# State increments in the four column quarters of the array, and a new issue table

## The chip, the cores and the metric

The kernel runs on one core of one Trainium2 chip. The metric is the device time of one execution in microseconds. TensorE (PE in the profile) does the matrix products, VectorE (DVE), ScalarE (ACT) and GpSimd (POOL) the elementwise work, and SyncE (SP) issues the transfers between memory and the core.

## What is computed

A linear attention with a decaying state, and behind it a gated feed-forward layer that mixes along the sequence. Cut to the core:

```python
# attention: 4 batches, 8 heads, 768 steps, head size 48
for t in range(S):
    cur = einsum('bhd,bhe->bhde', u * k[t], v[t])
    y[t] = einsum('bhd,bhde->bhe', r[t], state + cur)
    state = w[t][..., None] * state + einsum('bhd,bhe->bhde', k[t], v[t])
x = y as [4, 768, 384]
# gated layer: 384 -> 1024, halves u and v, mix along the sequence, 512 -> 384
h = maximum(x @ w_in, 0);  u, v = halves of h
v_n = (v - mean(v)) / sqrt(var(v) + 1e-6)
v_s = einsum('ts,bsd->btd', w_spatial, v_n) + b_spatial[None, :, None]
out = (u * v_s) @ w_out
```

## The kernel before

**Tiles.** The sequence of each batch is cut into 6 chunks of 128 steps, so there are 24 slots i (batch b, chunk c). In a slot the decay products come from two scans on DVE (`slot_prep`, lines 414 and 422: tiles `F` and `pa`), which scale `kk` and `rr`. Two heads stand one above the other in 112 partitions, so 4 pairs g cover the 8 heads.

**A slot on TensorE** is a row of blocks. `slot_kt` (L492) transposes `kk`. `slot_a` (L472, `pa<-rr,kk`) forms the scores of the chunk, both heads of a pair at once in two row halves of the array. DVE copies the masked scores into the tiles `As` (L477). `slot_y` (L512, output `pyw`) has three blocks: two *intra* blocks that multiply `As` with `v` (8 matmuls each) and, in all chunks but the first of a batch, an *inter* block with the state `Sd` (12 matmuls); their outputs are 32 columns wide, so four of them work side by side in the four column quarters of the array. `slot_s` (L550, `pd<-v,KT`) forms the state's increment: for each pair one product of 64 and one of 48 columns, side by side in two column halves, 8 matmuls in all. DVE, POOL and ACT then update the state `Sd` (L556 to L566). `slot_x` (L579 to L587) takes the output apart into a high and a low part.

**The gated layer on TensorE.** `hv_unit` (tile `ph`) forms the v half of a chunk, `g_unit` the u half (`pu`) and the mix along the sequence (`pv`), `out_unit` the last product (`po`). Each product is three matmuls with the full array (L592 to L594). The mix of a batch waits until all its six chunks are normalised (tiles `vh`, `vl`).

**Records.** A matmul of plain 32-bit floats stands in the profile as two records, one of the three of L592 to L594 as one. So the `pd` block is 16 records, an intra block 16, an inter block 24, a `pa` block 16.

**What sets the order.** All work is written down as 1805 operations with their dependences. `PLAN` has for each the engine it runs on (T, V, A, G, S for TensorE, DVE, ACT, POOL, SP) and a start time; `plan()` sorts by it, and each engine executes its own operations in just that order. An engine whose next operation isn't ready waits. Buffers are few (two each of `W`, `kk`, `rr`, `v`), so a load waits in SP's queue for the slot two before to be done with its buffer, and what stands behind it waits too.

**Filler.** `fill` puts matmuls on zeros (`warm`, L791, `pyw<-zk`) in the order wherever the table leaves TensorE idle for over 0.3 us, up to the operation `last`; they hold up TensorE's clock. They write a part of the tile `pyw`, in which the outputs stand.

The modes of the array are named in the code: `full` (128 by 128), `rows` (`pa`), `halves` (`pd`), `quadrants` (`pyw` of `slot_y`).

Of the kernel before, what the change touches and what calls it, by code (L numbers as in the profile page):

```python
# [15 lines left out]
B, H, S, D = 4, 8, 768, 48  # L16
# [3 lines left out]
R = 112  # L20
# [13 lines left out]
A31t V38b V3b7 V3qe A5sz V5zd S4hn V4t4 V5p1 V5tw V5vj A5yu G60x S3s4 A46d V4vn V5aj V5c6 A5eu G5gh S3bd
A3rr V4fl V4im V4wm A4zg G52v T1xf T2yw T30u A33g A35r A37u Sdt Sbp S9k Sjw Gli Tpr Vmc Vug Vv0 Vvk V120
A12k Gqx V12h Au1 Guw Gyk G10c T14z V1ba V18s Ttn V111 G124 A13p A14o Tvd Awz T1e2 T1fe T1go A1k9 T1m8 A1pe
T1zd T2wx T386 A3br A3fo A3gb Shr Ssp Sqk S19d G13j T18j V14d G17x V1at V1ep V1qb A1sg G18m V1i9 A1ct G1i9
G1ep G1gh T1re V1zr V21s Tz3 V17t G1c4 A1ja A1n0 T1cu A1eg T22e T27x T298 A2ck T2iv A2k0 T2uz T32t T34r A3ir
A3l2 A3lp A3t6 V4dc V4b3 G4bm V4du G4ee G4f1 V4gk A4h6 A4ng V4r7 V4k5 A4lr G4no V4h4 A4xr V50y S1b7 S1n1
S1it S1gy G1zr T241 V1t5 G23b V272 V27n V2b3 A2dw G272 V2bk A28a G1pc A28y A2g5 T2e3 V2in V2kn T1iw V1pc  # L40
G2gx A2lc A2mb T2bg V2dh T2lw T2na T2sr A2vp T37o A3vp T4b3 T4f0 T4gy A4jk A4tb A4tz S1kx S1xo S2bc S29e
G2k8 T2ov V2f7 V2yj V2z2 V2zn V353 A37a G326 V336 A2tf G2ic A2x1 G2yz T3ae V3gw V3dx T2h5 V2mo G30r V35o
A36b T36q A3aa T3xq T3z1 T40c A451 T4ei A4fu T4va T4x8 T4z7 A529 A54j A557 S2dg S2ix S2vf S2or G3dx T3i6
V3ix G3ns V3tv V3ux V3ug A3zw G3tv V3yg V3mg A30n A3o5 A40g T42k V492 V472 T3dg V3fx G3xe A4ev A442 T4kx
T4m8 T4nj A4qk T4us A4wf T515 T534 T552 A57o A59z A5am A5e1 G5dq V5fg V5g0 V5jw V5kf V5ky V5lh V5m1 A5oa
V5q2 V5nj A630 V659 A5m1 A5pz V5rz T5vo S3ly A3x1 S40n A4ao S4e0 A5ix S5ly A5vz T3ls T3n9 T45m A47s T5sr
T5u7 T60b T61s T6ew T6gd V6ih G6k4 A6n3 G6pp T3op T3q6 T4d1 A5hl T5xe T5yv T638 T64p T6aj T6ht V6k0 G6mx
A6pv G6si T3rm T3t3 T48j A4dj T5vy T6ja T6kq T6m7 T6nn T6p4 V6yh V7hn A7ly V7xl T3uj T3w0 T473 A497 T665
T67m T692 T6bz T6dg T6tq V75v G77x A7c4 V7u5 T80e T81v T83b T84s V87o S89e T7yy T8ki T8lz T8nf V8qt S8u5
T7xh T868 T87p T895 A8b9 S8cr T571 T58h T59y A5g9 T6v7 T6wn T6y4 T79a T7aq T7c7 V7oj V7z5 A84l V9co T5dm  # L50
T5f3 T5ij A61o T8ow T8qc T8uq T8y1 T8zi T90y V99d G9f8 A9it V9me T5k0 T5pu T5ra A5ue T9zu Ta1b Ta2r Ta48
Ta5o Taci Vaeo Gai7 Aal5 Gasc T5lg T5mx T5od A5ro T8rt T8t9 T9pn T9r3 T9sk T9u0 V9xi G9z5 Aa3u Va5i Ta93
Taux Tb6c Tb7t Ab9x Sbbe Tbo4 Tbpk Tbr1 Tbsh Vbul Sbwb Tas0 Tatg Tbuw Tbwc Abyg Sbzy S339 S3f0 S44a S5z0
S4ad V40j G472 V4ea V4ln V4ev A50v V455 V4p7 V6a9 V6bx V6dk G4ln A6f5 A6ir T4rq V6lk V6nk T4a0 V4bl T6qu
T6s5 A6u4 T6zk A70q T73e T75d T77b A79x A7dj A7e7 S3yj S46f S4pn S6f8 S4np V52v G58b V596 V6pl V59r A6t5
V56f V6t4 V712 V72q V74d A51f A75y G765 T70c V7a4 V783 T4j7 V4y6 G594 A5d2 V5x3 T5be V5dq T7dx T7f8 T7gj
A7j5 T7l4 A7nd T7qo T7sm T7vj A7y5 A80f A860 S4rr S4ws S4uo S761 S6vb V6v1 G6yl V701 V7ca V70l A7gn V7fq
V7j7 G7j7 G7m4 V7q3 G749 G80o A80z T7lw V898 V85n T5gt V5ix G6zd A7op A7po T7ir A7kh T8cm T8dx T8f8 A8jr
V8ma T92f T94d T96c A98y A9b8 A9gd A9lk V9ix V9ny G9r8 G9rv G9si Va72 Va7m Vad6 Aaer Vaoi Va9n Aab9 Gaeo
Va85 Aacy Gakz S6t7 S73a S7ju S7rr S7i1 V7l3 G7oy V7sk V8be V7vp A8ey G7pn V8ey V82g V844 V8ou G7vp G8qf  # L60
A8qf T8hg V8sd V8ue T7oy V7rl V7t6 A8ht A8is T7ul A7w6 T8wg T98k T99v A9nc V9ou Ta75 Taak Tbga Abl0 Abna
Abny S7fw S7ou S8hc S8qi S8jg V8gu V8nt V8od V8we V8qc A8zy V8ke V8zy G90j V95u V97v G8s7 G9aw A9bs T9l4
V9qe Vab5 T8aw V9aw V9e8 A9md A9fe Tahb Aaiw Tan6 Taoh Taps Aat1 Vav5 Tb2f Tb4e Tb99 Abbv Abe6 Abhl S8f0
S8la S9ez S99j S9d6 V91v V95e V97e V9sk V9oe A9w4 G97e V9z2 G9jk G9oe V9w0 G9t2 A9yx Aapf Tae9 Vaho Vat5
Talg Vanj Gav4 Vawq Vaxg Taxl Tayw Tb07 Ab2t Vb48 Tbi8 Tbk7 Tbm5 Abqe Abso Abtc Abvv Vc0z Vbyh Vbz1 Gc1h
Gc25 Gc2s Gc54 Acih Ackt Vcqn Acd3 Acfg Gchd Ac5u Ac87 Gca4 S9yb Aa8c Sabd Aamk Sapl Aazm Sb4g Abeq T9c3
T9dk T9vh A9xl Tckn Tcm3 Tcnk Tcuu Tcwb Tcxr Vd5s Vdfo Adlz Gdnm T9f0 T9gh T9hx A9k8 Tcqh Tcrx Tcte Tcz8
Td0o Td25 Vdh8 Ve5i Ae7g Vehp T9je T9wx T9ye Aa2i Tccx Td6r Td88 Td9o Te8k Tea0 Veci Gee6 Aeio Veks T9o6
Tai9 Tajp Aaud Tcee Tcfu Tcp0 Tdm8 Tdno Tdp5 Vdup Gdys Ae61 Vej9 Teom Tewb Tf3n Tf54 Vfbr Sfff Terj Tfzn
Tg13 Tg2k Vg8h Sga6 Tglp Tgn5 Tgom Tgq2 Vgs6 Sgtw Tbxt Tca0 Tcbh Ach5 Tefu Teha Telp Ten5 Teq2 Tfde Vffi  # L70
Vflk Afo4 Vfs9 Tbz9 Tc73 Tc8k Acb8 Tgrj Tgsz Tgug Th38 Th4o Th65 Vh89 Gh9w Ahij Ghml Tc0q Tc26 Tc3n Ac9w
Tgvw Tgzd Th0t Thg7 Thhn Thj4 Vhmw Vhpe Ahr1 Ghts Tdjb Tdkr Tebh Aedl Thbt Thda Theq Thkk Thm1 Thnh Vhqy
Vhy4 Aihs Gime Tiu3 Tivk Tix0 Tiyh Vj10 Sj2q Tisn Tj4b Tj5r Tjei Ajgm Sji4 Tir6 Tizx Tj1e Tj2u Aj5g Sj6y
S900 Sah7 Sat8 Sbip Savd Va0y Va4i Va51 Vajv Vb3n Ab48 Vaqf Vb1r Gbsq Gbvn Vbzh Gb3k Ac12 Gc3c Tbbi Vc4s
Vcda Tawd Aaxz Td3v Td56 Ad75 Vd9d Tdql Tdsk Tdui Adx4 Ae2x Ae3l S9w6 Sajb Sb2b Sc1s Sb0d Vb5r Vb9b Vbbn
# [47 lines left out]
Q = 32  # L123
# [802 lines left out]
```

## Time and profile before

| | |
|---|---|
| three runs | 387.41, 386.57, 386.63 us; median 386.63 |
| profiled execution, span | 386.2 us (the median of the runs is 0.4 us above it) |
| TensorE busy | 372.1 us, 96% |
| DVE, ACT, POOL busy | 260.1, 195.5, 140.2 us |
| filler records on TensorE | 128 of 3586 |
| instructions in the table on V, A, G, T, S | 468, 372, 180, 605, 180 |

The span reaches from the first to the last instruction. The profiler's records give the start and the end of each instruction; matmuls overlap, so the time that a block costs is read from its start to the start of the next block.

### The profile page before, as it was taken

To read this page: it belongs to the slowest core of one execution; us is meant where nothing else is said; L and a number is where in the kernel's file an instruction comes from. 1 tells how busy PE (TensorE), PEld (TensorE's weight loads), DVE (VectorE), ACT (ScalarE), POOL (GpSimd) and SP (SyncE) were. 2 spreads that over 40 slices of the span, in tenths; PEclk is the share of its full clock that TensorE was granted. 3 is DMA by queue.
4 is the path that set the end of the run, shared out by engine and by line. 5 is a ranking of instruction groups with operands and counts; after the bars stand their busy time and mean duration, and the time that the engine had idled before them with its cause. 6 is when DMAs were issued, how large, how long until landed. Compare 5 with 4: busy or idle time off the path is not lost.

```text
span 386.2 us, 9096 instructions
## 1 busy us (share of the span) xinstructions
PE 372.1 (96%) x3586; PEld 338.6 (88%) x3586; DVE 260.1 (67%) x477; ACT 195.5 (51%) x514; POOL 140.2 (36%) x195
## 2 busy tenths in 40 slices
PE   8989999999999999999999999999999999999993
PEld 7778797899888898799898989899998899999992
DVE  5879987878978886377887964775697525244240
ACT  2456588785563555772454544663146535641210
POOL 5656374413540634153543313442483003300010
PEclk9989999999999999999999999999999999999997
DMA  8988548614346336533453573132265410010102
GB/s 203 277 215 251 157 138 247 205 42 122 113 133 193 112 104 180 174 108 100 123 155 85 174 208 120 50 98 86 65 177 153 118 51 0 5 38 21 63 2 70
DMA packets 33011, 47.67 MB, mean 123 GB/s; under 512 B 3264, under 2 KB 21824, under 8 KB 32960
## 3 DMA queue, kind: packets, MB, share of 16 engines
q1 hardware_dynamic: 32960, 47.00, 41.6%
q8 instruction: 30, 0.49, 0.6%
q14 instruction: 21, 0.17, 0.2%
HBM read 42.27 MB, written 4.72 MB: 122 GB/s over the span
## 4 chain that ended last, share of the span: by engine, by line
PE 77%; DMA 11%; ACT 5%; DVE 3%; POOL 1%; issue 1%; SPq 0%; ACTq 0%; POOLq 0%; DVEq 0%
PE pv L592 9%; PE pv L594 8%; PE pv L593 8%; PE pyw L512 7%; PE pa L472 5%; DMA Nw<-in_gt_dram 5%; PE po L592 4%; PE po L594 4%; PE po L593 4%; PE pu L592 4%; PE ph L592 4%; PE pu L594 3%; PE pu L593 3%; PE ph L593 3%; PE ph L594 3%; PE pyw L791 3%
## 5 line engine op out<-in xcount | busy, mean ns | idle before, releaser
L592 PE MATMUL pv<-ws,vh 128*128 128x384 f32 x192 | 65.6, 342 | 0.0
L594 PE MATMUL pv<-ws,vl 128*128 128x384 f32 x192 | 64.4, 335 | 0.0
L593 PE MATMUL pv<-ws,vh 128*128 128x384 f32 x192 | 64.3, 335 | 0.0
L477 DVE COPY_PREDICATED As<-mask,pa 128x512 f32<-128x512 int32 x48 | 34.4, 731 | 10.3 <-PE pa L472 4.0
L592 PEld LDWEIGHTS pv<-ws,vh 128*128 128x128 f32 x192 | 36.0, 188 | 1.5 <-issue 0.6
L593 PEld LDWEIGHTS pv<-ws,vh 128*128 128x128 f32 x192 | 36.1, 188 | 0.2
L698 DVE TENSOR_TENSOR t<-pv,b_sb 128x384 f32<-128x384 f32 x32 | 17.7, 553 | 27.6 <-PE pv L594 27.3
L458 ACT ACTIVATE As<-ident,dg 128x128 f32<-128x128 f32 x100 | 31.8, 390 | 8.6 <-DVE dg L438 5.4
L594 PEld LDWEIGHTS pv<-ws,vl 128*128 128x128 f32 x192 | 36.0, 188 | 0.0
L414 DVE TENSOR_TENSOR_SCAN F<-zz,W 112x512 f32<-112x512 f32 x24 | 29.2, 1217 | 7.1 <-DMA W<-in_tr_dram 3.1
L592 PE MATMUL pu<-xT,wi 128*128 128x384 f32 x96 | 33.5, 349 | 0.1
L702 ACT CAST gh<-t 128x384 fp32r<-128x384 f32 x32 | 16.3, 510 | 33.9 <-DVE t L700 29.2
L592 PE MATMUL po<-wo,gh 128*128 128x384 f32 x96 | 33.1, 344 | 0.0
L594 PE MATMUL po<-wo,gl 128*128 128x384 f32 x96 | 32.3, 337 | 0.0
L594 PE MATMUL pu<-xT,wi 128*128 128x384 f32 x96 | 32.3, 336 | 0.0
L593 PE MATMUL po<-wo,gh 128*128 128x384 f32 x96 | 32.3, 336 | 0.0
L593 PE MATMUL pu<-xT,wi 128*128 128x384 f32 x96 | 32.2, 335 | 0.0
L592 PE MATMUL ph<-wi,xT 128*128 128x512 f32 x72 | 29.6, 411 | 0.9 <-ACT ph L624 0.9
L422 DVE TENSOR_TENSOR_SCAN pa<-zz,W 112x512 f32<-112x512 f32 x24 | 29.5, 1228 | 0.6
L593 PE MATMUL ph<-wi,xT 128*128 128x512 f32 x72 | 28.3, 393 | 0.0
L594 PE MATMUL ph<-wi,xT 128*128 128x512 f32 x72 | 28.3, 393 | 0.0
L453 POOL TENSOR_SCALAR_AFFINE_SELECT As<-dg 128x512 f32<-128x512 f32 x23 | 14.8, 648 | 36.8 <-DVE dg L438 15.8
(182 smaller groups left out, 856.3 us busy)
## 6 DMA issues: line engine op xcount, KB each, us to landing
N<-in_nat_dram SPq DMA_DIRECT2D x18, 384.0 KB, 3.1
Nw<-in_gt_dram SPq DMA_DIRECT2D x16, 384.0 KB, 3.6
W<-in_tr_dram SPq DMA_DIRECT2D x24, 224.0 KB, 3.1
kk<-in_tr_dram SPq DMA_DIRECT2D x24, 224.0 KB, 3.0
rr<-in_tr_dram SPq DMA_DIRECT2D x24, 224.0 KB, 3.4
v<-in_nat_dram SPq DMA_DIRECT2D x24, 192.0 KB, 3.5
out_dram<-ot SPq DMA_DIRECT2D x24, 192.0 KB, 2.7
wst<-in_w_spT_dram SPq DMA_DIRECT2D x12, 192.0 KB, 4.3
```

The costliest lines, as they stand in the source:

```text
L414: op({"V": 1.24}, lambda: nc.vector.tensor_tensor_scan(flat(F()[:R])[:, ::-1], flat(zz[:R])[:, ::-1], flat(W())[:, ::-1], 0.0, ALU.max, AL ...
L422: op({"V": 1.24}, lambda: nc.vector.tensor_tensor_scan(flat(E()[:R]), flat(zz[:R]), flat(W()), 0.0, ALU.max, ALU.mult), r=[(W, 0), ("zz", ...
L453: e.affine_select(out=As(), in_=dg()[:, j::2].unsqueeze(2).broadcast_to([P, G, C]), pattern=[[0, G], [1, C]], compare_op=ALU.is_equal, fil ...
L458: e.mul(As()[:, g, :], ident, dg()[:, 2 * g + j:2 * g + j + 1])
L472: nc.tensor.matmul(pa[j]()[:, g, :], kk()[rs, g, :], rr()[rs, g, :], start=True, stop=True)
L477: op({"V": 0.725}, lambda j=j, As=As: nc.vector.copy_predicated(As(), mask.unsqueeze(1).broadcast_to([P, G, C]), pa[j]()), r=[(pa[j], 0)], ...
L512: nc.tensor.matmul(py()[Q * n:Q * (n + 1), k_, :], a, b, start=n not in started, stop=not left[0], skip_group_check=True)
L592: nc.tensor.matmul(ps, ah, bh, start=first, stop=False)
L593: nc.tensor.matmul(ps, ah, bl, start=False, stop=False)
L594: nc.tensor.matmul(ps, al, bh, start=False, stop=last)
L698: op({"V": dve(HT)}, lambda: nc.vector.tensor_tensor(t1(), pv()[:, :HT], b_sb[:, tsl], ALU.add), r=[(pv, 0), ("b", 0)], w=[(t1, 0)])
L702: op({"A": act(HT)}, lambda: nc.scalar.copy(gh(), t1()), r=[(t1, 0)], w=[(gh, 0)])
```

## The change

Three things are edited. The increments `pd` are cut into pieces of at most 32 columns (32, 32, 32 and 16 for a pair), so that they use the four column quarters like the outputs: 16 matmuls instead of 8. The table `PLAN` is a list of operations in the order of issue instead of start times, and another order; it has the filler in it as words F with a count, and `fill` is gone. The planned costs of some TensorE blocks are other numbers; they are used by nothing in the kernel at run time.

```diff
 PLAN = """
-T0 S72 S8b S24n S266 S14i A1fx V1k5 V1le V1nf A1qq G1t5 Sut A16z V1ym V240 V2pp A2rq V2tj S1st A242 V25x
...
+Sq T0 Vw Sr Ss S2 S1 St Vx S42 A15 S41 S43 S1w Vy S2c Vu G12 Vz S44 V10 A11 V13 Fm Tv A14 V47 S55 T1b G17 T18
...
     def plan(self):
...
+        for w in PLAN.split():
+            if w[0] == "F":
+                order.append(int(w[1:], 36))
+            else:
+                o = self.ops[int(w[1:], 36)]
+                o.on = w[0]
...
-        op({"T": 1.0}, mm, r=[(kk, 0), (rr, 0), (rr, 1)], w=[(pa[0], 0), (pa[1], 0)], mode="rows")
+        op({"T": 0.89}, mm, r=[(kk, 0), (rr, 0), (rr, 1)], w=[(pa[0], 0), (pa[1], 0)], mode="rows")
...
         def mm():
             for g in range(G):
-                for j in range(2):
-                    hs = slice((2 * g + j) * D, (2 * g + j + 1) * D)
-                    rows = slice(64 * j, 64 + j * D)
+                for q4 in range(4):
+                    hs = slice((2 * g + q4 // 2) * D, (2 * g + q4 // 2 + 1) * D)
+                    rows = slice(Q * q4, min(Q * (q4 + 1), R))
                     nc.tensor.matmul(pd()[rows, g, :], KT()[:, g, rows], v()[:, hs], start=True, stop=True)
 
-        op({"T": 0.52}, mm, r=[(KT, 0), (v, 0)], w=[(pm_, 0), ("ds", i)], mode="halves")
+        op({"T": 0.4}, mm, r=[(KT, 0), (v, 0)], w=[(pm_, 0), ("ds", i)], mode="quadrants")
...
     def issue(order):
         for o in order:
-            o.fn(ENG[o.on]) if o.fn.__code__.co_argcount > len(o.fn.__defaults__ or ()) else o.fn()
-
+            if isinstance(o, int):
+                warm(o)
+            else:
+                o.fn(ENG[o.on]) if o.fn.__code__.co_argcount > len(o.fn.__defaults__ or ()) else o.fn()
...
-    def warm(us):
-        for _ in range(int(us)):
+    def warm(n):
+        for _ in range(n):
             nc.tensor.matmul(pw, zk, zk, start=False, stop=True, skip_group_check=True)
-
-    def fill(order):
-        t = first = 1.1
-        for o in order:
-            if o.on == "T":
-                if t < last.start and o.start - t > GAP:
-
-                    warm((o.start - t) * 1.2 / (0.214 if t > first else 0.43))
-                t = max(t, o.start + o.eng["T"])
-            yield o
```

The new table has 479 operations on DVE, 371 on ACT and 170 on POOL. Filler matmuls: 64 before, 33 now (23 ahead of the first work instead of 15, then 9, and one much later).

The first place is TensorE's order around the scores of slot 2 (`pa` of `rr_217` before, of `rr_246` now; `pd` is the increment of slot 2 in both, `pt` the transpose, `pyw<-zk` filler, `pyw<-xT` the low part of slot 1's output). Before:

```order
L550 MATMUL pd_395<-v_330,KT_357 48x48
L791 MATMUL pyw<-zk 128x128 x3
L582 MATMUL pyw<-xT_0_0_314,nident 128x384
L791 MATMUL pyw<-zk 128x128 x9
L472 MATMUL pa_0_359<-rr_217,kk_221 128x128
L472 MATMUL pa_1_440<-rr_217,kk_221 128x128
```

Now:

```order
L502 MATMUL pyw<-As_1_283,v_161 32x128 x4
L502 MATMUL pyw<-As_1_283,vp_114 32x128 x4
L502 MATMUL pyw<-rr_149,Sd 32x128 x12
L462 MATMUL pa_0_350<-rr_246,kk_254 128x128
L462 MATMUL pa_1_408<-rr_246,kk_254 128x128
```

The scores of slot 2 stood behind 12 filler matmuls and the product for slot 1's low part; now they follow the inter block of slot 1 directly.

The second place is the increment of slot 7 on TensorE (`pd`; `pu` are full-array products; `pyw<-As` the output of slot 6). The end of the increment and what follows, before:

```order
L550 MATMUL pd_1130<-v_1005,KT_1119 64x48
L550 MATMUL pd_1130<-v_1005,KT_1119 48x48
L592 MATMUL pu_1_1_1114<-xT_1_0_656,wi_117 128x384
L593 MATMUL pu_1_1_1114<-xT_1_1_824,wi_117 128x384
L594 MATMUL pu_1_1_1114<-xT_1_0_656,wi_118 128x384
```

Now:

```order
L540 MATMUL pd_1336<-v_1031,KT_1263 32x48 x3
L540 MATMUL pd_1336<-v_1031,KT_1263 16x48
L502 MATMUL pyw<-As_0_1293,v_888 32x128 x4
L502 MATMUL pyw<-As_0_1293,vp_113 32x128 x4
L502 MATMUL pyw<-As_1_1301,v_888 32x128 x4
L502 MATMUL pyw<-As_1_1301,vp_113 32x128 x4
L462 MATMUL pa_0_1320<-rr_1225,kk_1095 128x128
```

It stood alone between full-array products; now the output blocks of slot 6, in the same mode of the array, and the scores of slot 7 follow it directly. The mode of the array changes 122 times along TensorE's order before and 82 times now, 49 and 30 of these changes lead into `full`. From the first output block of slot 3 on it is 97 and 63, with 38 and 22 into `full`.

The third place is the order of loads on SP in the opening (`W`, `kk`, `rr`, `v` are loads of slots, `d_` are parts of the weights, 512 KB each). Before:

```order
L319 DMA d_('wu', 2)_189<-in_w_in_dram 128x1024
L369 DMA rr_217<-in_tr_dram 112x512
L369 DMA kk_221<-in_tr_dram 112x512
L319 DMA d_('wv', 1)_235<-in_w_in_dram 128x1024
L319 DMA d_('wu', 1)_274<-in_w_in_dram 128x1024
L319 DMA d_('wv', 0)_298<-in_w_in_dram 128x1024
L373 DMA v_330<-in_nat_dram 128x384
L366 DMA W_335<-in_tr_dram 112x4x128
```

Now:

```order
L356 DMA W_197<-in_tr_dram 112x4x128
L359 DMA rr_246<-in_tr_dram 112x512
L359 DMA kk_254<-in_tr_dram 112x512
L309 DMA d_('wv', 0)_272<-in_w_in_dram 128x1024
L309 DMA d_('wu', 1)_277<-in_w_in_dram 128x1024
L356 DMA W_286<-in_tr_dram 112x4x128
L363 DMA v_318<-in_nat_dram 128x384
L359 DMA kk_321<-in_tr_dram 112x512
```

Behind the loads of `rr` and `kk` for slot 2 stood three parts of the weights; now two stand there, and then the loads of slots 3 and 2.

## Rows read from the trace of the kernel before

**Rows 1.** The page: span, and busy time of each engine.
```profile
span 386.2 us, 9096 instructions
PE 372.1 (96%) x3586; PEld 338.6 (88%) x3586; DVE 260.1 (67%) x477; ACT 195.5 (51%) x514; POOL 140.2 (36%) x195
```

**Rows 2.** Stretches: us, busy time (instructions) by engine, clock, DMA share, GB/s.
```profile
0.00:10.00 10.00, 8.14 (x58) 7.97 (x58) 5.71 (x13) 3.16 (x9) 5.74 (x19) 1.00 0.83 202
10.00:41.36 31.36, 28.92 (x377) 24.27 (x373) 27.23 (x41) 15.60 (x41) 18.11 (x24) 0.95 0.84 244
41.36:85.60 44.24, 42.71 (x449) 37.69 (x448) 36.04 (x73) 35.62 (x95) 20.77 (x24) 1.00 0.55 161
85.60:379.70 294.10, 292.29 (x2711) 268.66 (x2709) 191.15 (x353) 140.64 (x370) 95.56 (x129) 1.00 0.35 103
```

**Rows 3.** Stretches of filler alone (line 791): PE, PEld, clock, DMA, GB/s.
```profile
10.00:41.36 31.36, 10.25 (x72) 8.79 (x72) 0.95 0.84 244
41.36:85.60 44.24, 3.61 (x27) 3.23 (x26) 1.00 0.55 161
```

**Rows 4.** Who TensorE's matmuls waited for: us in total, times, longest.
```profile
PE pyw L791 <- ACT xT L585: 1.2, 2, 0.6
```

**Rows 5.** TensorE in order of time: an increment between full-array products (start, us).
```profile
79.79 0.34 PE L594 MATMUL pu<-xT,wi 128*128 128x384 f32 x1
80.06 0.67 PE L550 MATMUL pd<-v,KT 128*64 128x48 f32 x16
80.66 0.44 PE L592 MATMUL pu<-xT,wi 128*128 128x384 f32 x1
80.94 0.34 PE L593 MATMUL pu<-xT,wi 128*128 128x384 f32 x1
81.11 0.34 PE L594 MATMUL pu<-xT,wi 128*128 128x384 f32 x1
```

**Rows 6.** TensorE from 116.9 us: an increment's start, and what still runs at 117.485.
```profile
116.92 0.67 PE L550 MATMUL pd<-v,KT 128*64 128x48 f32 x16
...
117.30 0.28 PE L550 MATMUL pd<-v,KT 128*64 128x48 f32 x2
```

**Rows 7.** Line 550: durations in ns, min/median/max; starts; forms.
```profile
L550 PE MATMUL pd<-v,KT x320: 208/222/343, 11.1 to 295.1; 128*48 128x48 f32 x81, 128*64 128x48 f32 x79
```

**Rows 8.** TensorE between 117.51 and 117.54 us: matmuls that begin in it.
```profile
117.51 0.32 PE L512 MATMUL pyw<-As,v 128*32 128x128 f32 x4
```

**Rows 9.** TensorE: an inter block, and the scores behind it.
```profile
118.41 0.84 PE L512 MATMUL pyw<-rr,Sd 112*32 112x128 f32 x24
119.18 1.16 PE L472 MATMUL pa<-rr,kk 48*128 48x128 f32 x16
```

**Rows 10.** A stretch of three output blocks in the opening: us, PE, clock, DMA, GB/s.
```profile
20.47:23.61 3.14, 3.14 (x57) 0.51 0.71 174
```

**Rows 11.** The chain that ended last, 8 to 30 us: start, us, what.
```profile
10.70 6.40 DMA kk<-in_tr_dram
...
17.23 1.28 POOL rk L396
...
26.27 2.27 PE pyw L791 x18
28.55 1.14 PE pa L472 x16
```

**Rows 12.** SP's issues in order of time, at 11.1 us.
```profile
11.12 0.43 SPq L319 DMA_DIRECT2D d_('wv', 1)_235<-in_w_in_dram  x1
```

**Rows 13.** The beginning: TensorE's filler and first work; DVE's first scan.
```profile
1.85 5.98 PE L791 MATMUL pyw<-zk 128*128 128x128 f32 x30 [1.85 <-DVE zz L261]
...
4.08 1.22 DVE L414 TENSOR_TENSOR_SCAN F<-zz,W 112x512 f32<-112x512 f32 x1 [2.27 <-DMA W<-in_tr_dram]
...
7.67 0.95 PE L401 MATMUL pg<-up_sb,rk 112*128 112x2 f32 x8
```

**Rows 14.** The end: the last copy of an output on ACT.
```profile
379.79 0.48 ACT L718 COPY ot<-po 128x384 f32<-128x384 f32 x1 [1.08 <-PE po L594]
```

More of the change, by code (lines that the diff above doesn't have):

```diff
@@ L34 @@
[L34 to L63, printed above, removed]
@@ new lines @@
+Sma Gk3 Vle Vkd Srk Tjj Vk8 Vl0 Tkg Vl3 Al1 Vl2 Tkh Gl9 Vqr Gqs Vqx Agv Agw Agx Sqq Tki Sqo Tla Amb Vqt Ai2 Vi4
+Gi3 Tna Smc Vi5 Amz Vi6 Vi7 Ajk Vi8 Tnb Tda Gi9 Skv Vlf Tdb Vig Alg Alh Via Tr8 Vlb Aih Tdc Vid Gdx Tdd Vlc Tnc
+Akj Vkk Aib And Amd Vii Gic Tde Tdf Tkl Aie Tkm Ajl Sme Vqu Vdg Vif Ar9 Ajm Srl Gl7 Tkn Vqy Ako Gdh Tli Tlj Adi
+Gdj Tlk Vqv All Srm Sro Vlm Ts6 Tr5 Ssq Tln Gr2 Akp Akq Vs7 Tlo Amf Ssp Tec Smg Aqw Vrp Vrv Grq Tlp Alq Sso Ted
+Tok Alr Als Tee Tef Aeg Vlu Alt Tol Vlv Teo Amh Tpc Tpd Sqp Vs8 As9 Glw Glx Vly Glz Vm0 Tom Vm4 Vm7 Tsb Asc Am5
@@ L143 @@
 class Op:
-    __slots__ = ("n", "eng", "fn", "pre", "suc", "bufs", "start", "on", "dma", "psum", "port", "mode")
+    __slots__ = ("n", "eng", "fn", "pre", "suc", "bufs", "on", "dma", "psum", "port", "mode")
 class Program:
@@ L188, in plan @@
     def plan(self):
-        words = PLAN.split()
-        assert len(words) == len(self.ops)
-        for o, w in zip(self.ops, words):
-            o.on, o.start = w[0], int(w[1:], 36) / 100
-            assert o.on in o.eng
-        return sorted(self.ops, key=lambda o: o.start)
+        order = []
+        for w in PLAN.split():
[4 more added lines that the diff above has]
+                o.on = w[0]
+                assert o.on in o.eng
+                order.append(o)
+        assert sorted(o.n for o in order if not isinstance(o, int)) == list(range(len(self.ops)))
+        return order
 def dve(n):
@@ L523, in slot_y @@
         for j in range(2):
-            op({"T": 0.47}, lambda j=j: intra(j), r=[(q["A", j], 0), (v, 0), ("vp", i % 2)], w=[(py, 0)],
+            op({"T": 0.45}, lambda j=j: intra(j), r=[(q["A", j], 0), (v, 0), ("vp", i % 2)], w=[(py, 0)],
                mode="quadrants")
@@ L530, in inter @@
                     mm(n, Sd[:, g, Q * m:Q * (m + 1)], rr()[:, g, :])
-            op({"T": 0.7}, inter, r=[(rr, 0), (rr, 1), ("Sd", 0), ("Sd", 1)], w=[(py, 0)], mode="quadrants")
+            op({"T": 0.57}, inter, r=[(rr, 0), (rr, 1), ("Sd", 0), ("Sd", 1)], w=[(py, 0)], mode="quadrants")
     def slot_s(i):
@@ L864 @@
         plan = prog.plan()
-        issue(fill(plan))
+        issue(plan)
     att.close()
```

121 lines of the change are left out of this document (65 added, 56 removed).

## The prediction

> **What bounds the kernel now.** I read the busy times first, then the stretches, then TensorE's waits and its order of time where the change touches it, and last the chain of waits in the opening and at the end.
>
> TensorE is busy for 372.1 of 386.2 us [rows 1]. From 85.60 to 379.70 us it works 292.29 of 294.10 us at the full clock [rows 2]: 1.8 us of waiting. DVE, the next engine, works 191.15 us there, 65%. So in three quarters of the run TensorE's own time is the run's time, and what is taken off a block there is taken off the end. Behind its last matmul come a copy, a store and the closing, from 379.79 to 386.2 us [rows 1, 14]; their order hardly changes, and I leave these 6.4 us as they are.
>
> The opening is different. TensorE begins with zeros at 1.85 us and has its first work at 7.67 us; DVE's first scan waits for a load until 4.08 us [rows 13]. From 10 to 41.36 us TensorE looks full (28.92 of 31.36), but 10.25 of it is filler [rows 2, 3]. DVE is busy for 27.23 us of that stretch, and for 5.71 us before it, so over the first 41.36 us it is idle for 8.4 us, 4.1 of them before its first scan. The opening is set by loads and by DVE's part of each slot. The border, 41.36 us, is where slot 3's first output block begins.
>
> **The change, term by term.** The sum runs from that border on, where TensorE decides, with the opening as one term. 16 of the 20 increments and, by the printed orders, 97 changes of the array's mode before against 63 now lie behind the border.
>
> *a. The increment itself.* The block at 116.92 us works in two column halves. At 117.485 us only matmuls of the 64-column half still run: two of them, first started at 117.30, together 0.28 us [rows 6]; one lasts 0.222 us, the line's median [rows 7], so they start 0.058 us apart, and the half's eight records span 0.47 us. The 48-column half is done by then, so its steps are at most 0.051 us: the step follows the columns. With quarters of 32 columns, eight records each, I take 0.047 us, a little under the 48-column step, as all pieces still pass 48 columns of `v`. The block falls from 0.47 to 0.38 us: 0.09 us each, 1.4 us for 16. Bounds: 0.06 us if the step stays 0.051 (1.0 us in all), 0.20 us if it falls with the columns to about 0.034 (3.2 us).
>
> The edit puts 32 records in place of 16, so the rate of records could bind. From 117.51 to 118.41 us two intra blocks, 32 records, take 0.90 us, 0.028 us each [rows 8, 9]; the 32 of an increment would take as long. But four matmuls to four column quarters begin between 117.51 and 117.54 us [rows 8], so records can begin within 0.01 us of each other, and I read the 0.028 us as the quarters' own step shared by four. The Trainium skill, "TensorE: Matmul & The Clock Gate", section "Wait — 56ns, not 53.3ns?", says that start-to-start never drops below about 25 ns however small a matmul is. By that the block would take 0.80 us, an estimate from the page's figure, and the sum below would end at 385 instead of 378.5 us. The row contradicts it for matmuls in different column quarters.
>
> *b. Changes of mode.* From the last full-array matmul to the increment it is 0.27 us (79.79 to 80.06), where full-array matmuls follow each other in 0.17 (80.94 to 81.11): 0.10 us for the change. The step of the first full-array matmul behind it is 0.28 us (80.66 to 80.94), 0.11 more than the usual one, and the increment's end costs as much again as its beginning (0.60 us from start to start for a block whose records span 0.47) [rows 5]. So a change costs 0.10 us, and one into the full array another 0.11. The scores behind an inter block show the like: the inter block takes 0.77 us from 118.41, its 24 records at 0.028 would take 0.67 [rows 9]. 34 changes fewer behind the border, 16 of them into the full array, are 3.4 + 1.8 = 5.2 us. This is the largest term, and it rests on TensorE being the bound there.
>
> *c. Filler behind the border.* 27 records, 3.61 us of busy time [rows 3], about 3.1 us from start to start as they overlap; one matmul of 0.14 us is left. They stand where the old table saw TensorE idle, so part of them becomes waiting. But they also delay work: filler writes the output tile and waits for ACT to have read it, 1.2 us in two waits [rows 4]. I take half, 1.5 us; bounds 0 and 2.9.
>
> *d. The opening.* Two things speak for a gain. In the old chain the load of `kk` for slot 2 takes 6.40 us from 10.70 [rows 11], with three weight parts of 512 KB issued right behind it (the first at 11.12 [rows 12]) on engines that are busy for 0.84 of the time [rows 2]; the multiply on POOL starts only at 17.23. In the new order that load stands before two parts instead of three. And 18 filler records, 2.27 us from 26.27, stand on the chain directly before the scores of slot 2 at 28.55 [rows 11]; the new order has none there. Against it: 46 filler records instead of 30 open the run. The last 16 cost 0.126 us each at the full clock (2.27 / 18), so the first work comes at about 9.7 us instead of 7.67, and 2 us late are the scores of slot 0, for which DVE and two buffers wait. DVE has nearly the same operations to do up to slot 3's scores in both orders, so its 4.3 us of idle time behind the first scan are the most that can be gained. I take 1.5 us; bounds 4.3 gained and 2 lost.
>
> *e. New waits.* The old order waits 1.8 us behind 85.60. The new one gives DVE, ACT and POOL 7 us less of TensorE work to hide behind, puts the blocks of a slot directly behind each other, so that one late tile stops them all, and moves work to DVE (479 operations against 468). I add 1.5 us; bounds 0 and 4.
>
> Sum: -1.4 - 5.2 - 1.5 - 1.5 + 1.5 = -8.1 us. Against the profiled execution this is 378.1 us of span; with the 0.4 us between span and median, and from the median, 386.6 - 8.1 = **378.5 us**. With all bounds good it would be 371, with all bad 386.4.
>
> **Rivals.**
>
> *Eaten up.* The blocks get cheaper but the opening and the waits take half or more of it: 382 to 385.9 us. For it: DVE is busy for 27.23 of 31.36 us in the opening and 36.04 of 44.24 behind it [rows 2], so it can become the bound up to 85 us; the opening filler is longer. Against: behind 85.60 it has a third of its time free. Chance 0.18.
>
> *More in the opening.* All of d and c come in, the step of a falls with the columns: 371 to 375 us. Chance 0.10.
>
> *Records bind.* 32 records at 0.028 us: the block takes 0.90 instead of 0.47 us, 0.43 x 16 = 6.9 us more instead of 1.4 less, so 378.5 + 8.3 = 386.8 us, no change. The four starts within 0.03 us speak against it [rows 8]; 0.05. The page's 25 ns, with the same mechanism, gives 385 and lies within this case.
>
> *The clock falls: slower.* Of 64 filler matmuls 31 go, and the opening's real work is thin. Three output blocks took 3.14 us at a granted clock of 0.51 [rows 10]; the like blocks take 1.67 us at the full clock (117.51 to 119.18 [rows 8, 9]). With the increment behind them such a stretch loses about 1.8 us. To eat 8.1 us and 0.8 more it takes five stretches more than before, all where TensorE decides. For it: with 9 filler matmuls left between 10 and 41 us, TensorE has some 19 us of real work in those 31 us, and the clock can fall in any of its pauses. Against: in the opening, DVE and the loads wait less for TensorE than it for them, so half speed there is partly hidden; behind 41 us the work is dense and the clock was 1.00 throughout [rows 2]. 0.09; about 388 to 392 us.
>
> **How the numbers follow.** My forecast, 375 to 382 us, has 0.58. With 0.18 at 382 to 385.9, 0.10 at 371 to 375, 0.05 about the old time and 0.09 above, the range that leaves out no more than 2 in 10 goes from 372.5 to 385 us: 0.06 below, 0.14 above. A difference under 0.2% (0.8 us) can't be told from none. Faster by more: 0.58 + 0.10 + 0.18 = 0.86. Within it: 0.06, most of it from the record rate. Slower: 0.08.
>
> **What would show it.** a: a `pd` block of 32 records over about 0.6 us from first start to last end, and starts of four within 0.03 us. b: 82 changes; `pd` blocks between `pyw` and `pa` with about 0.1 us at each border, and the count of matmul steps of 0.27 to 0.28 us among the full-array ones down by a third. c: behind the border hardly any filler, and waits of TensorE there under 4 us. d: first work near 9.7 us, but slot 3's first output block at 40 us or before. e: behind 85 us TensorE idle for no more than 3.5 us, and its last matmul at 371 to 372 us.
>
> It would be wrong if TensorE shows long waits at the groups of a slot (for `As`, `Sd` or `kk`), if the granted clock stands at 0.5 in several slices of the first fifth, or if slot 3 begins later than at 44 us: each of these costs more than the term that it stands against.

## The result, and the profile after

| | before | after |
|---|---|---|
| four runs, median | 386.60 us (385.99 to 387.41) | 374.61 us (373.35 to 376.50) |
| ratio of the times | | 0.9693, 95% interval 0.9654 to 0.9732 |
| the same in another session (11 and 6 runs) | 386.99 us | 373.99 us; 0.9697 (0.9657 to 0.9736) |
| profiled execution, span | 386.2 us | 374.7 us (a run of 376.50 us, the longest of the four) |

The kernel is 12 us faster. I had forecast 8.1: the time lies in my range (372.5 to 385.0 us), 0.4 us below the likeliest case (375 to 382) and so in the rival "more in the opening" (371 to 375). The page of after begins with the span and the busy time of each engine:

```profile
span 374.7 us, 9569 instructions
PE 357.9 (96%) x3844; PEld 332.2 (89%) x3844; DVE 261.1 (70%) x488; ACT 186.9 (50%) x498; POOL 147.7 (39%) x185
```

TensorE has 258 records more than before [rows 1] and 14 us less busy time. The next view gives busy times by stretch, for after: up to the first work, up to slot 3's first output block (the border), up to the first product of the mix (`pv`), and up to the last matmul. The columns are start:end, length, busy time (instructions) of PE, PEld, DVE, ACT and POOL, clock, DMA share and GB/s.

```profile
0.00:9.64 9.64, 7.79 (x47) 7.79 (x47) 4.88 (x13) 2.15 (x5) 3.18 (x16) 1.00 0.74 201
9.64:35.40 25.76, 23.89 (x422) 20.69 (x420) 23.07 (x36) 16.50 (x46) 17.70 (x19) 0.93 0.79 232
35.40:79.80 44.40, 39.24 (x420) 34.16 (x420) 39.60 (x76) 31.64 (x87) 18.58 (x23) 0.92 0.64 189
79.80:367.77 287.97, 286.98 (x2961) 269.54 (x2960) 193.43 (x365) 136.15 (x361) 108.25 (x129) 1.00 0.36 107
```

The same view of before, with its own first `pv` at 84.41 us:

```profile
41.36:84.41 43.05, 41.52 (x441) 36.50 (x440) 34.88 (x71) 34.49 (x93) 20.77 (x24) 1.00 0.56 165
84.41:379.71 295.30, 293.49 (x2717) 269.85 (x2716) 192.31 (x355) 141.78 (x372) 95.56 (x129) 1.00 0.35 103
```

The border comes 5.96 us earlier (41.36 to 35.40). The stretch from there to the first `pv` is 1.35 us longer. The long rest is 7.33 us shorter (295.30 to 287.97), and the closing behind the last matmul 0.4 us longer. Two things are to be seen in the third line of after: TensorE is busy for 39.24 of 44.40 us, so it waits; and DVE is busy for 89% where it was 81%. The waits of TensorE, in order of size:

```profile
PE pt L482 <- issue: 2.8, 1, 2.8
PE pyw L502 <- DVE As L467: 1.9, 1, 1.9
...
PE pv L582 <- DVE S L548: 1.0, 1, 1.0
```

The first two lie between the border and the first `pv`; the third is all that is left behind it. In order of time (start, duration), with what the granted clock does about them:

```profile
35.64 0.40 PE L502 MATMUL pyw<-As,vp 128*32 128x128 f32 x8
37.95 0.66 PE L502 MATMUL pyw<-As,v 128*32 128x128 f32 x8 [1.91 <-DVE As L467]
...
62.22 0.40 PE L584 MATMUL ph<-wi,xT 128*128 128x512 f32 x1
65.43 0.98 PE L482 MATMUL pt<-ident,kk 112*128 112x112 f32 x4 [2.81 <-issue]
```

```profile
20.70:24.40 3.70, 3.70 (x66) 3.30 (x61) 3.63 (x7) 1.60 (x5) 2.00 (x3) 0.54 0.62 173
37.80:41.40 3.60, 3.45 (x43) 2.74 (x44) 3.06 (x9) 1.68 (x5) 0.00 (x0) 0.53 0.63 163
65.10:68.80 3.70, 3.37 (x56) 2.96 (x60) 3.63 (x9) 0.94 (x2) 0.38 (x1) 0.54 0.15 29
```

Three stretches stand at about half the clock (1.2 of 2.4 GHz), where before had one [rows 10]. The first follows a stretch with small waits (17.40 to 20.90 us: busy for 2.67 of 3.50), the other two begin where the two long waits end.

On DVE and POOL, this is what stands before the ends of the two waits:

```profile
34.40 1.09 POOL L417 TENSOR_TENSOR kk<-kk,F 112x508 f32<-112x508 f32 x1
34.52 2.74 DVE L328 SCALAR_TENSOR_TENSOR e_('wv', 1)_480<-d_('wv', 1)_352,e_('wv', 1)_480 128x512 int32<-128x512 int32 x1
37.18 0.72 DVE L467 COPY_PREDICATED As<-mask,pa 128x512 f32<-128x512 int32 x1
...
64.65 0.68 DVE L417 TENSOR_TENSOR kk<-kk,F 112x508 f32<-112x508 f32 x1
```

The copy that ends the first wait stands behind a conversion step of a weight part that took 2.74 us, where the same step of two other parts took 0.68 and 0.66. It began 0.12 us after a multiply on POOL. In the run with the shorter start (the last of the experiments) it began 0.03 us before that multiply, and took 0.67 us:

```profile
32.02 0.67 DVE L326 SCALAR_TENSOR_TENSOR e_('wv', 1)_472<-d_('wv', 1)_344,e_('wv', 1)_472 128x512 int32<-128x512 int32 x1
32.05 1.58 POOL L415 TENSOR_TENSOR kk<-kk,F 112x508 f32<-112x508 f32 x1
```

There this wait is not in the list. So the wait comes from one slow step more than from the amount of work; that POOL's head start is the reason is not tested by itself. For the second wait the profile names no releaser ("issue"); the multiply on DVE that writes `kk` ends 0.10 us before the transpose begins.

Last, the increments, which [rows 5] and [rows 6] show before. First slot 7's, between a full-array product and the output blocks; then slot 9's, between two output blocks of its own mode:

```profile
93.82 0.34 PE L584 MATMUL pv<-ws,vl 128*128 128x384 f32 x1
94.09 0.54 PE L540 MATMUL pd<-v,KT 128*32 128x48 f32 x32
94.46 0.40 PE L502 MATMUL pyw<-As,v 128*32 128x128 f32 x8
...
116.50 0.40 PE L502 MATMUL pyw<-As,vp 128*32 128x128 f32 x8
116.71 0.52 PE L540 MATMUL pd<-v,KT 128*32 128x48 f32 x32
117.05 0.84 PE L502 MATMUL pyw<-rr,Sd 112*32 112x128 f32 x24
```

From start to start 32 records take 0.34 us (116.71 to 117.05) with no change of mode on either side, and 0.37 with one ahead (94.09 to 94.46); before, 16 records and a change behind them took 0.60 (80.06 to 80.66 [rows 5]).

### The profile page after: what moved, and what is told of

The parts are those of the page before. It is cut to its first block, busy times and chain, and to the rows that moved or that the text cites. A ratio compares the mean times of both kernels' runs of the same rounds, so it can differ in the third digit from the quotient of the medians.

```text
span 374.7 us, 9569 instructions
## 1 busy us (share of the span) xinstructions
PE 357.9 (96%) x3844; PEld 332.2 (89%) x3844; DVE 261.1 (70%) x488; ACT 186.9 (50%) x498; POOL 147.7 (39%) x185
## 4 chain that ended last, share of the span: by engine, by line
PE 85%; DVE 10%; issue 2%; ACT 1%; POOL 0%; DVEq 0%; POOLq 0%; ACTq 0%
PE pyw L502 9%; PE pv L582 9%; PE pv L584 9%; PE pv L583 9%; PE pa L462 6%; PE po L582 4%; PE pu L582 4%; PE po L584 4%; PE po L583 4%; PE pu L584 4%; PE pu L583 4%; PE ph L582 4%; PE ph L584 4%; PE ph L583 4%; PE pyw L783 3%; PE pt L482 2%
## 5 line engine op out<-in xcount | busy, mean ns | idle before, releaser
L443 POOL TENSOR_SCALAR_AFFINE_SELECT As<-dg 128x512 f32<-128x512 f32 x28 | 21.6, 780 | 40.8 <-DVE dg L428 10.7
L448 ACT ACTIVATE As<-ident,dg 128x128 f32<-128x128 f32 x80 | 25.5, 392 | 19.1 <-DVE dg L428 15.6
L690 POOL TENSOR_TENSOR t<-t,us 128x384 f32<-128x384 f32 x16 | 17.4, 1089 | 40.4 <-DVE t L688 24.7
L582 PE MATMUL po<-wo,gh 128*128 128x384 f32 x96 | 32.9, 342 | 0.0
L582 PE MATMUL ph<-wi,xT 128*128 128x512 f32 x72 | 29.5, 410 | 0.0
L462 PE MATMUL pa<-rr,kk 48*128 48x128 f32 x384 | 28.3, 287 | 0.2 <-PE pt L482 0.2
```

The lines of the kernel that those rows point to most:

```text
L443: e.affine_select(out=As(), in_=dg()[:, j::2].unsqueeze(2).broadcast_to([P, G, C]), pattern=[[0, G], [1, C]], compare_op=ALU.is_equal, fil ...
L448: e.mul(As()[:, g, :], ident, dg()[:, 2 * g + j:2 * g + j + 1])
L462: nc.tensor.matmul(pa[j]()[:, g, :], kk()[rs, g, :], rr()[rs, g, :], start=True, stop=True)
L582: nc.tensor.matmul(ps, ah, bh, start=first, stop=False)
L690: op({"V": dve(HT), "G": pool(HT)}, lambda e: e.tensor_tensor(t1(), t1(), us(), ALU.mult), r=[(us, 0)], w=[(t1, 0)], port=True)
```

## The experiments

The kernels of one session share a chip and the runs of before (medians 387.42, 387.54 and 386.99 us). To write old and new order in one form, the old table was rewritten as a list of words; its order on each engine is the old one. In every trace I also read the time from the first `pv` to the last matmul, because that stretch has the full clock and little waiting, and repeats: 287.97 and 287.93 us in two executions of after.

**The increment alone, in the old order.**

```diff
-                    rows = slice(64 * j, 64 + j * D)
+                    rows = slice(Q * q4, min(Q * (q4 + 1), R))
```

> The old order, with the increments in four column quarters; nothing else is changed. By my forecast's terms 0.09 us for each of the 16 blocks behind the border (1.4 us), and 7 of the 97 changes of mode there fall away (those between an increment and an output block), 0.10 us each (0.7 us): 2.1 us faster than before, 384.5 us. By the trace of after (an increment takes 0.34 us from start to start between blocks of its own mode, 0.48 in halves) it is 16 x 0.14 + 7 x 0.115 = 3.0 us: 383.6 us. If records bound the block, 6.9 us slower. If the increment is not on the path in the old order, no change.

384.15 us, ratio 0.9924 (0.9892 to 0.9956): 3.3 us faster by the medians, 2.9 by the ratio. From the first `pv` it is 292.28 us, 3.02 less than before. An increment that stays between blocks of other modes takes 0.47 us there in place of 0.595. Records do not bind.

**The old increment in the new order.**

```diff
-                    rows = slice(Q * q4, min(Q * (q4 + 1), R))
+                    rows = slice(64 * j, 64 + j * D)
```

> The new order, with the increments in two column halves as before. 17 changes of mode more behind the border, 80 in place of 63, and 16 dearer blocks. By the forecast's terms 16 x 0.09 + 17 x 0.10 = 3.1 us slower than after: 377.7 us. By the steps of the trace of after 16 x 0.14 + 17 x 0.115 = 4.2 us: 378.8 us. If the time came from the opening and the loads alone, under 1 us slower: 374.6 to 375.6 us.

377.83 us, ratio 0.9749 (0.9715 to 0.9783): 2.0 us slower than after by the ratios, 3.2 by the medians. From the first `pv` it is 290.60 us, 2.63 more. By the steps in this trace the 14 blocks there and their borders cost 3.8 us more; 1.0 of it is covered, since TensorE's wait for DVE's `S` at a `pv` (1.0 us in after) is gone, and TensorE is busy for the whole 290.60 us.

Together with before and after, these two runs make a square. From the first `pv` to the last matmul the old order takes 295.30 us, and 292.28 with quarters; the new order takes 290.60, and 287.97 with quarters. There the quarters are worth 3.0 us in the old order and 2.6 in the new one, the order 4.7 us without them and 4.3 with them: two nearly independent gains.

**The new order up to the border, the old one behind it (with quarters).** The list is cut at its 160th operation:

```diff
 ... G7y A77 F1 T8f S8z
-Vg F1 T7z S2l V7a A75 T7i T7j Vl ...
+S29 A2a S23 G75 A24 A27 S3 ...
```

> Quarters, the new order for the first 160 operations on all engines (up to about the border), and the old order with its filler behind them. If TensorE decides from the border on and the opening is worth what the border shows, it is faster than the old order with quarters by the 6.0 us by which the border came earlier: 377.6 us. If the opening is worth what I forecast, by 1.5 us: 382 us. If the old order behind the border waits for DVE and the loads just as long, it gains nothing on the old order with quarters: 383.6 us.

388.99 us, ratio 1.0017 (0.9984 to 1.0049): 4.8 us slower than the old order with quarters. The border comes at 34.09 us, earlier than in after, and the gain is lost at once:

```profile
38.36 0.40 PE L582 MATMUL ph<-wi,xT 128*128 128x512 f32 x1
45.19 0.80 PE L580 MATMUL ph<-wi,xT 128*128 128x512 f32 x1 [6.43 <-ACT wi L327]
```

The conversion that this product waits for stands on ACT behind that of another weight part, whose load lands at 44.08 us. So the joined list makes a wait of its own, and the run doesn't price the opening. What it does show: an early border is no gain as long as work that was put off for it is still to come.

**The new order up to 97 us, the old one behind it (with quarters).** The same, cut at the 510th operation.

> Quarters, the new order for the first 510 operations (up to about 97 us), and the old order behind them. 84 changes of mode behind the border, 34 into the full array, where the new order has 63 and 22. If the order of the dense part is worth its changes of mode, it is slower than after by 21 x 0.105 + 12 x 0.11 = 3.5 us: 378.1 us. If the changes cost nothing and the gain was made before 97 us, it is as fast as after: 374.6 us.

381.15 us, ratio 0.9832 (0.9793 to 0.9870): 6.5 us slower than after by the medians, 5.3 by the ratios, more than the 3.5 us that I expected of the changes of mode. Up to the first `pv` it is as fast as after (79.99 us); from there it is 294.92 us, 7.0 more. TensorE is busy for 291.79 of it, 4.8 more than in after, so 3.1 us are waits, against 1.0: the new dense order saves 4.8 us of TensorE's time, where I had 3.5 for the changes, and 2 us of waiting as well.

**The old order without the filler behind the first word.**

```diff
-A4q F4 T4j
+A4q T4j
...
-V1s F9 T5n
+V1s T5n
...
```

> The kernel before with all filler taken out but the 15 matmuls ahead of the first work and the one behind the mix's first tiles. If the filler was in the way of real work, 3 us behind the border and up to 4 us of the 9.4 us (from start to start) before it are gained: 380 to 384 us. If it stood in idle time and held the clock up, the waits stay, the clock falls in more stretches than one, and each costs about 1.7 us: 386.6 to 392 us.

385.42 us, ratio 0.9948 (0.9916 to 0.9981): 2.1 us faster. 12.4 us of filler (from start to start) are gone, and some 10 us come back as waits and as half clock:

```profile
17.30:24.20 6.90, 6.76 (x84) 5.85 (x84) 4.17 (x8) 3.67 (x9) 4.15 (x7) 0.51 0.83 251
27.50:31.00 3.50, 3.24 (x21) 2.09 (x21) 3.07 (x6) 1.45 (x3) 2.47 (x4) 0.51 0.89 255
37.80:48.10 10.30, 9.73 (x84) 7.62 (x81) 8.38 (x19) 5.18 (x14) 4.08 (x5) 0.50 0.46 134
```

Both cases of the expectation are half right: some filler was in the way, and the clock did fall, in 20 us of the first 48. Ahead of the first `pv` TensorE is idle for 8.4 us in place of 5.8, so most of what came back is time at half the clock; how much of it would have been waiting at the full clock is not shown.

**Filler in the two long waits.**

```diff
-T7i T7j
+T7i F8 T7j
...
-T8t Tfg
+T8t Fb Tfg
```

> The new kernel with filler in the two longest waits of TensorE: 8 matmuls in the wait for slot 3's second block of scores (35.8 to 37.9 us), 11 in the wait for slot 6's transpose (62.4 to 65.4 us). Behind each the granted clock was at one half for some 3.4 us. If the idle time brings the clock down, both stretches are at the full clock and 1.5 to 1.7 us are won for each that is on the path: 371.2 to 373 us. If the clock falls for another reason, or the stretches are hidden behind DVE, no change: 374.6 us; if the filler delays the work behind it, up to 1 us slower.

374.52 us, ratio 0.9660 (0.9623 to 0.9698), which can't be told from after. The clock did as expected in both stretches:

```profile
37.80:41.40 3.60, 3.50 (x53) 2.59 (x53) 3.44 (x10) 1.96 (x5) 0.50 (x1) 1.00 0.92 234
...
65.10:68.80 3.70, 3.66 (x109) 3.29 (x109) 3.63 (x8) 2.40 (x6) 0.00 (x0) 1.00 0.23 56
```

Its first `pv` comes at 78.01 us, against 79.80 in the first profile of after and 76.84 in the second. So of the 3.1 us that the two stretches cost TensorE only a part can reach the end of the run: by the ratios the gain is 1.3 us, not clear of none. That the rest is hidden, because a faster TensorE waits longer for DVE, is how I read it.

**The price of a change of mode.** 20 matmuls of filler, each between two output blocks (two changes of mode, one into the full array), and, to compare, each between full-array products:

```diff
-Tkh
+F1 Tkh
```

> The new kernel with 20 single filler matmuls of the full array behind 90 us, each between two output blocks of the same mode, so that each adds two changes of mode, one of them into the full array. 20 matmuls cost 2.7 to 5 us by themselves (0.14 to 0.25 us each by the filler of the two traces). By the forecast's terms 20 x 0.31 = 6.2 us on top: 383.5 to 386 us. If a change of mode costs nothing, 377.3 to 379.6 us, the same as with 20 between full-array matmuls.

> The new kernel with the same 20 filler matmuls behind 85 us, each between two full-array matmuls, so that no change of mode is added. 2.7 to 5 us slower than after: 377.3 to 379.6 us. The difference to the run with the same matmuls between output blocks is the price of 40 changes of mode.

388.03 us, ratio 0.9990 (0.9959 to 1.0022), and 379.45 us, ratio 0.9806 (0.9766 to 0.9846). From the first `pv` it is 299.76 and 293.01 us: 6.75 us apart, 0.34 us for each of the 20 places, where I had 0.31 for a pair of changes. The first run lies above what I expected: 11.8 us more than after in this stretch, in place of 8.9 to 11.2. (The medians lie 8.6 us apart; the profile between output blocks has two more stretches of half clock in the opening.) The two surroundings, first between output blocks:

```profile
117.65 0.43 PE L500 MATMUL pyw<-As,v 128*32 128x128 f32 x8
117.90 0.40 PE L500 MATMUL pyw<-As,vp 128*32 128x128 f32 x8
118.23 0.49 PE L781 MATMUL pyw<-zk 128*128 128x128 f32 x2
118.65 0.43 PE L500 MATMUL pyw<-As,v 128*32 128x128 f32 x8
```

Then between full-array products:

```profile
164.09 0.34 PE L582 MATMUL pv<-ws,vl 128*128 128x384 f32 x1
164.27 0.38 PE L781 MATMUL pyw<-zk 128*128 128x128 f32 x2
164.41 0.42 PE L580 MATMUL pv<-ws,vh 128*128 128x384 f32 x1
164.67 0.34 PE L581 MATMUL pv<-ws,vh 128*128 128x384 f32 x1
```

Between output blocks the same matmul holds the array for 0.42 us (118.23 to 118.65), between full-array ones for 0.14 (164.27 to 164.41). But there the first product behind it has a step of 0.26 in place of 0.17 us (164.41 to 164.67), with no change of mode. So 0.34 us is not the price of a pair: the run that it is compared with pays 0.09 us of its own at each place. By the rows the pair costs 0.11 us ahead of the filler (0.33 from 117.90 to 118.23, where 0.22 is usual), 0.28 on it and 0.02 behind it (118.65 to 118.89, where 0.22 is usual), some 0.41 us. That is another make-up than around an increment. After has the long first step behind transposes too: they also use the full array, stand as one record each, and in seven places the first product behind them has 0.26 us.

**After once more, a shorter start, less work on DVE, and a combination.** The start has 14 filler matmuls in place of 22 (`Fm` becomes `Fe`); the combination has this start and the filler in the two waits. For less work on DVE, three steps of the conversion of `wu` and `wo` are cut:

```diff
-            op(us, lambda e: f(e, *parts()), r=[(d, 0)], w=[(em, 0)], port=port)
+            op(us, lambda e: f(e, *parts(n if few or key[0] == 'wv' else n // 8)), r=[(d, 0)], w=[(em, 0)], port=port)
```

> The changed kernel once more, beside the three others on the same chip: 374.6 us again by its first four runs (373.3 to 376.5).

> The changed kernel with 14 filler matmuls in place of 22 in the word that opens TensorE's order, which brings its first work back to about 7.7 us. By my term on the opening, which charges the longer filler with 2 us, up to 2 us faster than after: 372.6 us. If loads and DVE set the opening and TensorE's first scores have slack, no change: 374.6 us. If the shorter filler brings the clock down once more in the opening, up to 1.7 us slower: 376.3 us.

> The changed kernel with three of the conversion steps of the weight parts wu and wo on an eighth of their columns, so that those weights are not converted rightly: some 6 us less work on DVE, most of it between 25 and 80 us; nothing on TensorE changes. If DVE sets the path between the border and the mix, the waits of TensorE for the scores of slot 3 (2.1 us) and the transpose of slot 6 (3.0 us) shrink, and the run is 3 to 5 us faster than after: 369.6 to 371.6 us. If those waits are for loads, no change: 374.6 us.

> The run with filler in the two waits (8 and 11 matmuls) and with 14 filler matmuls in place of 22 at the start. If the filler in the waits is worth the 1.8 us by which its profiled execution ended earlier, 372.8 us, and 370.8 us if the start is worth 2 us as well; if the stretches of half clock are mostly hidden behind DVE and the start has slack, within 0.8 us of after: 373.8 to 375.4 us.

| kernel | median, us | ratio to before (95%) | first `pv` at, us |
|---|---|---|---|
| after again | 373.99 | 0.9697 (0.9657 to 0.9736) | 76.84 |
| shorter start | 373.12 | 0.9665 (0.9624 to 0.9706) | 76.35 |
| less work on DVE | 371.44 | 0.9615 (0.9580 to 0.9650) | 76.54 |
| shorter start and filler | 372.72 | 0.9640 (0.9608 to 0.9673) | 77.15 |

The shorter start brings the first work to 8.01 us and can't be told from after in time: the medians lie 0.9 us apart and the intervals overlap, so the 2 us that I charged are neither shown nor ruled out. The combination has the lowest median of the kernels that do all the work, 1.3 us under after, but the intervals overlap; it isn't shown to beat after.

Less work on DVE is faster, 2.6 us by the medians, 3.2 by the ratios, as expected if DVE sets the path. The wait for slot 6's transpose is gone; the one for `As` is 1.3 us, with the slow step there too (2.17 us). From the border to the first `pv` its clock is 1.00 throughout, as in the run with filler in the waits, so the two can be compared there. First the one with filler, then the one with less DVE work:

```profile
35.37:78.01 42.64, 41.15 (x458) 36.09 (x458) 39.58 (x76) 31.89 (x87) 18.63 (x23) 1.00 0.69 200
```

```profile
38.41:76.54 38.13, 36.39 (x421) 31.76 (x420) 31.79 (x76) 31.81 (x87) 16.73 (x22) 1.00 0.73 216
```

With 7.8 us less on DVE the stretch is 4.5 us shorter. Part of this is its later start: this execution has the half clock from 21.1 to 31.3 us, its border comes 3.0 us later, and its first `pv` only 1.5 us earlier. So DVE is on the path in this stretch, but this pair doesn't price it, and the profiled run is the longest of its six (373.64 us).

The second profile of after shows how the same kernel differs from run to run:

```profile
26.50:30.10 3.60, 3.60 (x82) 3.21 (x85) 3.57 (x7) 1.18 (x2) 3.37 (x3) 0.53 0.71 215
50.40:54.00 3.60, 3.58 (x19) 3.51 (x12) 3.53 (x11) 3.60 (x13) 0.63 (x3) 0.53 0.73 260
```

Here two stretches of half clock lie elsewhere, the border is at 36.75 us, and the wait for slot 6's transpose, 2.8 us in the first profile, is no longer in the list of waits. The order of the opening is the same; what waits in it, and where the clock is low, differs from one execution to the next.

## Why the prediction was right, and where it was off

For each term I take the first profile of after against before. For b and e, I took the time from start to start of every TensorE block behind the border, and subtracted the median of the same kind without a change of mode beside it (0.52 us for three products of `pu`, `pv` or `po`, 0.69 for `ph`, 0.44 and 0.66 for an intra and an inter block, 0.32 for a transpose). What is over at changes is b, what is over elsewhere is e. Scores have a change on both sides in either order and count alike. The two stretches at half the clock, 3.1 us dearer than at the full clock, lie partly in b and partly in e.

| term, us | forecast | measured |
|---|---|---|
| a, the increment | -1.4 | -2.2 (16 x 0.14) |
| b, changes of mode behind the border | -5.2 | -5.0 (15.2 to 10.2) |
| c, filler behind the border | -1.5 | -2.9 (3.05 to 0.14) |
| e, waits behind the border | +1.5 | +5.2 (4.0 to 9.2) |
| d, opening | -1.5 | -6.0 at the border |
| ahead of the border in the new order: one block more of `pg` (the term with `u`) and one product for a low part | 0 | -0.9; -0.2 |
| closing behind the last matmul | 0 | +0.4 |
| sum | -8.1 | -11.6 (by the spans -11.5) |

**a** was right in mechanism and a little small. The pieces of 32 columns start 0.0425 us apart in a quarter (0.34 / 8), not 0.047, which makes 0.34 against 0.48 us (0.595 less 0.115 for the change behind it). The rival that records bind falls: 32 records in 0.34 us are 0.011 us each, 0.021 for a matmul. The Trainium skill, "TensorE: Matmul & The Clock Gate", section "Wait — 56ns, not 53.3ns?", has about 25 ns as the least distance of two starts; the trace does not agree for matmuls in different column quarters.

**b** was right in size. The old increment in the new order and the new increment in the old order both moved as the steps of the trace of after say. The single filler matmuls don't confirm the price: 0.41 us for their pair, of another make-up, against 0.31. One step of its reading was wrong. I put 0.11 us down to a change "into the full array"; the filler between full-array products shows 0.09 us more for the first product behind it without any such change. Behind transposes it is the same. So that part comes with another kind of matmul ahead of the product; since a transpose is a single record too, the number of records alone isn't the reason, and which property is stays open. It didn't matter for the sum, as both happen at the same places.

**c** and **e** belong together, as I had them; c came in whole, and e is beyond its bound of 4. Behind the first `pv` the waits did not grow but shrank (TensorE idle for 1.0 us; before it was 1.8). They grew between the border and the first `pv`, where my list of what would prove it wrong had put them: long waits for `As` and for slot 6's `kk`, and stretches at half the clock. These signs came and the forecast held all the same, since c and d brought more than they cost.

**d** is the term that was mis-sized: 1.5 us, with a bound of 4.3. I had counted only DVE's idle time in the opening as gain, since "DVE has nearly the same operations to do up to slot 3's scores in both orders". That step failed. DVE is busy for 32.9 us before the border in the old order (5.71 and 27.23 [rows 2]) and for 27.95 in the new (4.88 and 23.07): 5 us less. By the view by lines, the largest parts of it are two steps of a fourth weight part (2.4 us), now done behind the border, the copies of two transposes (1.2 us), now on ACT, and one copy of scores (0.7 us). The bound was also misread: 0.8 us of the 4.1 before the first scan is work (tiles set to zero), so the idle time behind it was 5.1 us, not 4.3.

But the 5 us belong to this pair of executions. DVE's order is the same in before, in the old order with quarters and in the old order without filler. The same view up to the border, first for after, then for these two:

```profile
0.00:35.40 35.40, 31.68 (x466) 28.48 (x466) 27.95 (x48) 18.65 (x51) 20.88 (x35) 0.95 0.78 224
0.00:43.97 43.97, 37.37 (x495) 33.07 (x495) 29.36 (x53) 18.64 (x49) 23.03 (x42) 0.92 0.81 220
0.00:39.50 39.50, 31.57 (x360) 26.14 (x360) 27.90 (x52) 18.13 (x48) 23.86 (x42) 0.85 0.87 244
```

With the old order DVE is busy for 29.36 and 27.90 us there, 0 to 1.4 us more than in after, and the border still comes at 43.97 and 39.50 us. These kernels differ from before in the increments or in the filler, but not in what DVE does. So neither the time that DVE works nor its idle time follows from its order, and no bound on the gain could be read from one trace. How much of the 6 us is less work, and how much less waiting, stays open. Part of it is given back up to the first `pv`, since there DVE is on the path, as the run with less work on DVE shows: the first `pv` comes 4.6 us earlier in the first profile (84.41 to 79.80) and 7.6 in the second (76.84). In the two other traces of the old order it comes at 87.18 (with quarters) and 82.47 (without filler). The rival "eaten up" had this mechanism right and its size too large.

The rival "the clock falls" came in part: two stretches of half clock more in the first profile. They cost TensorE some 1.6 us each, near the 1.8 that I reckoned, but with both at the full clock the run can't be told from after; that they lie where TensorE waits for DVE anyway is the likely reason.

The rival "more in the opening" is where the time ended, by 0.4 us, and with part of its mechanism: c and d came in whole, d beyond its bound at the border; the step of a fell only to 0.0425 us, not to 0.034. That my sum missed by no more than 3.5 us is in part luck: c and d brought 5.9 us more than I had, and e took 3.7 back. Of the signs that I had named, the first work at 9.64 us, the 82 changes and the early border came; the last matmul ended before 371 us, at 367.77, and TensorE waited 6.1 us behind the border, not under 4.

What stays open: how much of the opening's gain is due to the order of the loads and how much to the order on DVE. The run that was to split the opening off brought a wait of its own.

## What to carry to other kernels

Where TensorE decides, count the changes of the array's mode and of the kind of matmul along its order, and put blocks of one mode side by side; a change and its way back cost 0.3 to 0.4 us here, as much as the small block itself. An event that comes earlier is no gain by itself: add up what each engine has still to do behind it, and look which engine is the bound there. Filler shows where an engine was idle, not what removing it brings: taken out alone, four fifths of it came back, as waits and as half clock. And read an opening from several executions: two of one kernel had their first `pv` 3 us apart.

## What the runs showed of the hardware

- Matmuls of 48 columns in four column quarters pass at 0.011 us per record, 0.021 us per matmul.
- The first single-record product behind plain 32-bit matmuls has a step of 0.26 in place of 0.17 us, with no change of mode (164.41 to 164.67 us); so has the first product behind a transpose.
- What a change of mode costs depends on what is under way: 0.10 us behind a full-array product, 0.11 behind an increment or an output block, and 0.28 behind a single filler matmul of the full array (0.42 less 0.14).
- The granted clock of one kernel falls at other places from run to run: at 20.9, 37.9 and 65.2 us in one execution of after, at 26.6 and 50.5 in the next.
- One conversion step on DVE took 2.74 us when it began 0.12 us after a multiply on POOL, and 0.67 us when it began 0.03 us before it; POOL's multiply then took 1.58 in place of 1.09 us.
